# First batch of an attention-then-phase-MLP kernel loaded with two tokens per partition and put in token order by selection products; the channel weight's cast moved to another engine

**Chip, cores, metric.** One core of one Trainium2 chip. The metric is the device time of one execution in microseconds (us), the median of several; lower is better. The span of a profile (first to last instruction) is about 1.8 us shorter than the time of the same run. A second state, slower by some per cent at a lower clock, turns up in some executions of any kernel. e5 to e8 ran on chip 8, the other experiments on chip 14, each beside runs of the kernel before on its own chip. In the traces PE is TensorE, DVE VectorE, ACT ScalarE, POOL GpSimd and SP SyncE, which issues the transfers (DMA); PSUM is the memory into which PE's products go (tiles named ..._ps), and evacuation is the copy out of it.

## The reference, cut to what matters

Four batches of 768 tokens, eight heads of 64. A retention layer (a running state per head that decays by gamma and takes up k v at each token) gives x; x goes through a phase MLP whose token mixing needs all 768 tokens of a batch.

```python
for t in range(S):                       # retention
    state = gamma * state + k[t] (outer) v[t]
    y[t] = scale * q[t] @ state
x = y, heads side by side                # (4, 768, 512)
theta = x @ w_theta
zr, zi = x * cos(theta), x * sin(theta)
u = x + w_tok_r @ zr + w_tok_i @ zi      # over the tokens of one batch
out = u + relu(u @ w_ch)
```

## The kernel before: the parts that matter

A token tile is 128 tokens; there are 24, six to a batch. "Prologue" is batch 0 (tiles 0 to 5), after which a loop of slots takes a tile a slot and, beside it, the token mixing of output tiles.

```python
def load_chunk(n):                       # one tile: 64 floats = 256 bytes a row
    for name, src in (("kf", k), ("qf", q), ("vf", v)):
        t = io.tile([P, H, D], FT, name=name, bufs=9)
        nc.sync.dma_start(out=t, in_=src[b, :, c*P:(c+1)*P, :].rearrange("h s d -> s h d"))
...
def att_prep(n):                         # GpSimd: to bf16, with decay factors
    nc.gpsimd.tensor_copy(kb, kf); nc.gpsimd.tensor_mul(qb, qf, qsc); nc.gpsimd.tensor_mul(vb, vf, vsc)
def att_T(n):                            # k and q transposed, ONE VectorE copy of 128x1024
    ...
    nc.vector.tensor_copy(kqT, kq_ps)
def att_A(n):                            # k q^T of eight heads, masked, one PSUM buffer
    at_ps = psum.tile([P, 2, NP, P], FT, name="at_ps", tag="at", bufs=1)
    ...
    nc.vector.tensor_mul(at, at_ps, mask)
# att_Y: y^T and the state; att_X: x, theta, cos and sin (ScalarE); att_Z: z = x*(cos, sin) (VectorE)
...
for s_ in range(last_slot):              # the slot loop
    ...
    if s_ == 0:
        w_cast(3)
        nc.gpsimd.tensor_copy(wch, wdma["ch"])   # channel weight, 128x2048
    if s_ + 1 in n_of and n_of[s_ + 1] < N_DMA:
        att_prep(n_of[s_ + 1])           # GpSimd, behind that cast
```

## Time and profile before

| | value |
|---|---|
| time, median (3 runs) | 183.64 us (181.92 to 552.78; the last is an outlier) |
| time and span of the profiled run | 185.79 and 184.0 us |
| busy in that span: PE, VectorE, ScalarE, GpSimd | 161.1, 106.1, 72.6, 79.9 us |
| transposes of tile 6 (the prologue's last act) | 41.65 us |
| transposes of tile 8 (slot loop running free) | 54.89 us |
| from tile 6's transposes to the end | 142.35 us |

PE is busy in 88% of the span; of its 22.9 us of idle time 17.1 lie in the first 60 us and 3.9 in the last 5. Between them PE simply works, so the kernel is read by milestones: when PE starts the transposes of a given tile. Whatever delays tile 8 delays the end.

### The profile page before, as it was taken

What the parts mean: (1) busy time and instruction counts of PE and PEld (TensorE: products, weight loads), DVE (VectorE), ACT (ScalarE), POOL (GpSimd) and SP (SyncE); (2) the same over time, 40 slices, a digit from 0 to 9 for tenths busy, and PEclk for the clock granted to TensorE, in tenths of its full rate; (3) what the DMA queues carried; (4) which work ended last, traced back from release to release, by engine and by line L of the source; (5) the groups of instructions that cost most, each with busy time, mean ns of one, the idle gap of its engine ahead of it and who ended that gap; (6) DMA issues with size and microseconds to landing.
All of it is one profiled execution on the core that took longest, in us unless ns stands there. A gap on an engine that the chain in (4) does not pass through costs nothing.

```text
span 184.0 us, 3550 instructions
## 1 busy us (share of the span) xinstructions
PE 161.1 (88%) x1392; PEld 91.6 (50%) x1392; DVE 106.1 (58%) x146; ACT 72.6 (39%) x136; POOL 79.9 (43%) x105
## 2 busy tenths in 40 slices
PE   0567997795499989799999999999999999999991
PEld 0244655452265656555655565555545544444560
DVE  1264684736155877868976686756556634534442
ACT  4052754640044645554734544265354342200010
POOL 4648767691977669655859455231000000000000
PEclk9999999999579999999999999999999999999998
DMA  6999999998999989999999999954483333334343
GB/s 133 222 316 218 227 254 279 284 286 242 229 279 218 288 177 222 257 277 231 242 210 254 260 224 188 203 143 114 110 108 100 101 85 77 107 118 114 111 122 116
DMA packets 95265, 35.63 MB, mean 194 GB/s; under 512 B 89488, under 2 KB 89744, under 8 KB 95248
## 3 DMA queue, kind: packets, MB, share of 16 engines
q1 hardware_dynamic: 95104, 35.27, 85.4%
q8 instruction: 11, 0.18, 0.5%
q10 hardware_dynamic: 144, 0.13, 0.2%
q14 instruction: 6, 0.05, 0.1%
HBM read 25.69 MB, written 6.29 MB: 174 GB/s over the span
## 4 chain that ended last, share of the span: by engine, by line
PE 63%; SPq 15%; DMA 9%; DVE 5%; POOL 3%; ACT 1%; issue 1%; DVEq 0%; POOLq 0%
PE y_ps L282 29%; SPq L80 12%; PE o_ps L310 10%; PE th_ps L253 8%; DMA w<-in_moe_w_ch_dram 5%; DMA wtok<-in_moe_w_tok_r_dram 3%; PE at_ps L185 3%; PE yT_ps L214 3%; PE kq_ps L165 3%; SPq L94 2%; PE st_ps L222 2%; DVE at L189 2%; PE x_ps L250 2%; PE yT_ps L203 2%; DMA uT<-u 2%; DVE z L264 1%
## 5 line engine op out<-in xcount | busy, mean ns | idle before, releaser
L282 PE MATMUL y_ps<-z,wtr 128*128 128x512 bf16 x138 | 53.1, 385 | 1.5 <-DVE z L264 1.0
L282 PE MATMUL y_ps<-z,wti 128*128 128x512 bf16 x138 | 53.1, 385 | 0.0
L189 DVE TENSOR_TENSOR at<-at_ps,mask 128x1024 bf16<-128x1024 f32 x24 | 29.3, 1220 | 9.4 <-PE at_ps L185 9.4
L258 ACT ACTIVATE cs<-th_ps,halfpi 128x512 bf16<-128x512 f32 x24 | 16.5, 687 | 38.5 <-PE th_ps L253 38.5
L264 DVE TENSOR_TENSOR z<-cs,x_sb 128x1024 bf16<-128x1024 bf16 x24 | 20.8, 865 | 15.1 <-ACT cs L259 15.0
L154 POOL TENSOR_TENSOR kqb<-qf,qsc 128x512 bf16<-128x512 f32 x24 | 25.2, 1052 | 8.9 <-DMA qf<-in_q_dram 8.7
L156 POOL TENSOR_TENSOR vb<-vf,vsc 128x512 bf16<-128x512 f32 x24 | 25.4, 1060 | 7.5 <-PE yT_ps L214 3.3
L253 PE MATMUL th_ps<-wth,xT 128*128 128x512 bf16 x96 | 25.5, 389 | 1.9 <-DVE wth L393 1.9
L168 DVE COPY kqT<-kq_ps 128x1024 bf16<-128x1024 bf16 x19 | 13.1, 689 | 21.0 <-PE kq_ps L165 21.0
L153 POOL CAST kqb<-kf 128x512 bf16<-128x512 f32 x24 | 16.4, 684 | 18.8 <-DMA kf<-in_k_dram 8.1
L165 PE MATMUL kq_ps<-ident,kqb 128*128 128x128 bf16 x152 | 13.9, 238 | 11.7 <-POOL kqb L153 8.8
L287 DVE TENSOR_TENSOR u<-y_ps,x_sb 128x512 bf16<-128x512 f32 x23 | 15.8, 689 | 13.7 <-PE y_ps L282 13.7
L310 PE MATMUL o_ps<-wch,uT 128*128 128x512 bf16 x92 | 23.5, 380 | 0.1
L231 ACT CAST xT<-yT_ps 128x512 bf16<-128x512 f32 x24 | 14.0, 585 | 24.1 <-PE yT_ps L214 24.0
L313 DVE SCALAR_TENSOR_TENSOR ot<-o_ps,u 128x512 f32<-128x512 f32 x23 | 15.8, 690 | 10.2 <-PE o_ps L310 10.1
L282 PEld LDWEIGHTS <-wti 128*128 128x128 bf16 x138 | 13.6, 99 | 15.5 <-issue 2.6
L282 PEld LDWEIGHTS <-wtr 128*128 128x128 bf16 x138 | 13.6, 99 | 14.1 <-DVE wtr L334 0.7
L165 PEld LDWEIGHTS <-kqb 128*128 128x128 bf16 x152 | 11.0, 106 | 16.8 <-POOL kqb L153 9.2
L259 ACT ACTIVATE cs<-th_ps,zerob 128x512 bf16<-128x512 f32 x24 | 16.3, 680 | 0.0
L236 ACT CAST stbd<-st_ps 64x256 bf16<-64x256 f32 x40 | 14.7, 366 | 0.5
L295 ACT COPY uT<-u_ps 128x512 bf16<-128x512 bf16 x12 | 7.0, 585 | 18.5 <-PE u_ps L293 18.5
L310 PEld LDWEIGHTS <-uT 128*128 128x128 bf16 x92 | 8.7, 98 | 9.8 <-DMA uT<-u 0.3
(51 smaller groups left out, 149.0 us busy)
## 6 DMA issues: line engine op xcount, KB each, us to landing
kf<-in_k_dram SPq DMA_DIRECT2D x24, 256.0 KB, 4.8
qf<-in_q_dram SPq DMA_DIRECT2D x24, 256.0 KB, 5.1
vf<-in_v_dram SPq DMA_DIRECT2D x24, 256.0 KB, 5.3
out_dram<-ot SPq DMA_DIRECT2D x23, 256.0 KB, 2.2
wtok<-in_moe_w_tok_r_dram SPq DMA_DIRECT2D x6, 384.0 KB, 5.3
wtok<-in_moe_w_tok_i_dram SPq DMA_DIRECT2D x6, 384.0 KB, 5.1
w<-in_moe_w_theta_dram SPq DMA_DIRECT2D x1, 1024.0 KB, 6.7
w<-in_moe_w_ch_dram SPq DMA_DIRECT2D x1, 1024.0 KB, 8.5
```

The source lines that it names most:

```text
L80: nc.sync.dma_start(out=t, in_=src[b, :, c * P:(c + 1) * P, :].rearrange("h s d -> s h d"))
L153: nc.gpsimd.tensor_copy(kb.rearrange(r3, h=H), raw[n, "kf"])
L154: nc.gpsimd.tensor_mul(qb.rearrange(r3, h=H), raw[n, "qf"], _bcast_last(qsc[:, c], D))
L156: nc.gpsimd.tensor_mul(vb.rearrange(r3, h=H), raw[n, "vf"], _bcast_last(vsc[:, c], D))
L165: nc.tensor.transpose(kq_ps[:, i * NP + j, :], src[:, j * P:(j + 1) * P], ident)
L189: nc.vector.tensor_mul(at.rearrange("p a j t -> p (a j) t"), at_ps.rearrange("p a j t -> p (a j) t"), _bcast_mid(mask, H))
L253: nc.tensor.matmul(th_ps, s["xT"][:, j, :], wth[:, j, :], start=(j == 0), stop=(j == NP - 1))
L258: nc.scalar.activation(cs[:, 0, :], th_ps, AF.Sin, bias=halfpi, scale=1.0)
L259: nc.scalar.activation(cs[:, 1, :], th_ps, AF.Sin, bias=zerob, scale=1.0)
L264: nc.vector.tensor_mul(zs[b][:, c], st[n]["cs"], _bcast_mid(xs[b][:, c, :], 2))
L282: nc.tensor.matmul(y_ps, wT[r][:, s0, t0 * P:(t0 + 1) * P], zs[b][:, s0, r, :], start=(s0 == 0 and r == 0), stop=(s0 == nT - 1 and r == 1))
L310: nc.tensor.matmul(o_ps, mo[m]["uT"][:, j, :], wch[:, j, :], start=(j == 0), stop=(j == nD - 1))
```

## The change

The intent: rows of 512 bytes should cost the DMA engines less per byte than rows of 256. So k, q and v of batch 0 are loaded two tiles at a time, with tokens 2p and 2p+1 of 256 in partition p. For k and v the token order is restored by products with a 0/1 selection matrix (sel) into PSUM, for the transposed k and q by a copy that interleaves the even and odd tokens. v goes on ScalarE's queue. The prologue is reordered for pairs, and the cast of the channel weight goes from GpSimd in slot 0 to ScalarE in slot 2. To make room the single-tile load buffers go from 9 to 7 for each tensor and the buffers of the two 1 MB weights from 2 to 1. The diff is cut and shortened.

```diff
+    def load_pair(g, names, eng):
+                t = io.tile([P, H, 2 * D], FT, name="pair", bufs=5)
+                eng.dma_start(out=t, in_=src[0, :, 2*g*P:2*(g+1)*P, :].rearrange(
+                    "h (p two) d -> p h (two d)", two=2))
-    for what in ("c0 c1 th c2 c3 c4 w0 c5 w1 w2 c6 w3 ch c7 c8 ...
+    load_pair(0, "v", nc.scalar)
+    loads("p0 th p1 w0 p2 w1 w2 c6 w3 c7 ch c8 ...")
...
+    def pair_T(g, name):                 # for k, then for q
+        ps = psum.tile([P, NP, 2, P], BF, name="kq_ps", tag="tr", bufs=2)
+        ... transposes ...
+        nc.vector.tensor_copy(t.rearrange("d j (p two) -> d j p two", two=2),
+                              ps.rearrange("d j two p -> d j p two"))
+    def pair_rows(g, name):              # for k, then for v
+        ps = psum.tile([P, 2, dm], FT, name="r_ps", tag="at", bufs=1)
+        ... four products: sel[rows, two] with the landed rows into ps[:, a] ...
+        for a in range(2):
+            if name == "v" and a == 0: nc.vector.tensor_copy(t, ps[:, a, :])
+            else:                      nc.scalar.copy(t, ps[:, a, :])
...
+    def pair_in(g):
+        pair_prep(g, "k"); pair_T(g, "k"); pair_rows(g, "k")
+        pair_prep(g, "q"); pair_T(g, "q")
+        if g > 0: att_Z(2 * g - 1)
+        att_A(2 * g)
+        pair_prep(g, "v"); pair_rows(g, "v")
+        att_A(2 * g + 1)
+    pair_in(0); att_YS(0); ... load_pair(1, "v", nc.scalar); att_X(0); att_YS(1) ...
-            nc.gpsimd.tensor_copy(wch, wdma["ch"])          # slot 0
+        if s_ == 2: wch_cast(0, nD)                         # four ScalarE copies
-    ... O_at = ... {2: 0, 3: 1}
+    ... O_at = ... {3: 0, 4: 1}                             # o of the first two output tiles a slot later
```

More of the change, by code (lines that the diff above doesn't have):

```diff
@@ L78, in load_chunk @@
         for name, src in (("kf", k), ("qf", q), ("vf", v)):
-            t = io.tile([P, H, D], FT, name=name, bufs=9)
+            t = io.tile([P, H, D], FT, name=name, bufs=7)
             nc.sync.dma_start(
@@ L82, in load_chunk @@
             raw[n, name] = t
+    def load_pair(g, names, eng):
+        for name, src in (("k", k), ("q", q), ("v", v)):
+            if name in names:
+                t = io.tile([P, H, 2 * D], FT, name="pair", bufs=5)
+                eng.dma_start(out=t, in_=src[0, :, 2 * g * P:2 * (g + 1) * P, :].rearrange(
+                    "h (p two) d -> p h (two d)", two=2))
+                raw[g, name] = t
     wdma = {}
     def load_w512(name, src):
-        t = io.tile([P, nD, dm], FT, name="w512", bufs=2)
+        t = io.tile([P, nD, dm], FT, name="w512", bufs=1)
         nc.sync.dma_start(out=t, in_=src.rearrange("(a p) e -> p a e", p=P))
@@ L95, in load_wtok, with loads @@
         wdma[r, t0] = t
-    for what in ("c0 c1 th c2 c3 c4 w0 c5 w1 w2 c6 w3 ch c7 c8 w4 c9 c10 w5 c11 "
-                 "c12").split():
-        if what == "th":
-            load_w512("th", moe_w_theta)
-        elif what == "ch":
-            load_w512("ch", moe_w_ch)
-        elif what[0] == "c":
-            load_chunk(int(what[1:]))
-        else:
-            for r in range(2):
-                load_wtok(r, int(what[1:]))
+    def loads(order):
+        for what in order.split():
+            if what == "th":
+                load_w512("th", moe_w_theta)
+            elif what == "ch":
+                load_w512("ch", moe_w_ch)
+            elif what[0] == "w":
+                for r in range(2):
+                    load_wtok(r, int(what[1:]))
+            elif what[0] == "p":
+                load_pair(int(what[1:]), "kq", nc.sync)
+            else:
+                load_chunk(int(what[1:]))
+    load_pair(0, "v", nc.scalar)
+    loads("p0 th p1 w0 p2 w1 w2 c6 w3 c7 ch c8 w4 c9 c10 w5 c11 c12")
     posn = const.tile([P, nT], FT)
@@ L127 @@
     nc.scalar.activation(qsc, arg, AF.Exp, bias=lscale, scale=1.0)
+    posp = const.tile([P, nT], FT)
+    nc.gpsimd.iota(posp, pattern=[[2 * P, nT // 2], [1, 2]], base=1,
+                   channel_multiplier=2, allow_small_or_imprecise_dtypes=True)
+    argp = const.tile([P, nT, H], FT)
+    nc.vector.tensor_mul(argp, _bcast_last(posp, H), _bcast_mid(lg, nT))
+    vscp = const.tile([P, nT, H], FT)
+    nc.scalar.activation(vscp, argp, AF.Exp, bias=zerob, scale=-1.0)
+    qscp = const.tile([P, nT, H], FT)
+    nc.scalar.activation(qscp, argp, AF.Exp, bias=lscale, scale=1.0)
     ident = const.tile([P, P], BF)
@@ L133 @@
                             base=0, pattern=[[1, P]], channel_multiplier=-1)
+    sel = const.tile([P, 2, P], BF)
+    nc.gpsimd.memset(sel, 1.0)
+    for a in range(2):
+        half = sel[a * P // 2:(a + 1) * P // 2]
+        nc.gpsimd.affine_select(out=half, in_=half, compare_op=ALU.is_equal, fill=0.0,
+                                base=0, pattern=[[1, 2], [-1, P]], channel_multiplier=2)
     stbd = []
@@ L151, in att_prep @@
         kb, qb = kqb[:, 0, :], kqb[:, 1, :]
-        vb = work.tile([P, dm], BF, name="vb", bufs=5)
+        vb = work.tile([P, dm], BF, name="vb", bufs=8)
         nc.gpsimd.tensor_copy(kb.rearrange(r3, h=H), raw[n, "kf"])
@@ L168, in att_T @@
         nc.vector.tensor_copy(kqT, kq_ps)
-        s["kqT"] = kqT
+        s["kT"], s["qT"] = kqT[:, 0:NP, :], kqT[:, NP:2 * NP, :]
     def att_T_dma(n):
@@ L175, in att_T_dma, with pair_prep @@
             out=kqT, in_=s["kqb"].rearrange("p a d -> p (a d)"))
-        s["kqT"] = kqT
+        s["kT"], s["qT"] = kqT[:, 0:NP, :], kqT[:, NP:2 * NP, :]
+    def pair_prep(g, name):
+        t = work.tile([P, 2, dm], BF, name="kqb", bufs=5)
+        src = raw[g, name].rearrange("p h (two d) -> p two h d", two=2)
+        dst = t.rearrange("p two (h d) -> p two h d", h=H)
+        if name == "k":
+            nc.gpsimd.tensor_copy(dst, src)
+        else:
+            for two in range(2):
+                sc = (qscp if name == "q" else vscp)[:, 2 * g + two]
+                nc.gpsimd.tensor_mul(dst[:, two], src[:, two], _bcast_last(sc, D))
+        st[g, name] = t
+    def pair_T(g, name):
+        ps = psum.tile([P, NP, 2, P], BF, name="kq_ps", tag="tr", bufs=2)
+        for two in range(2):
+            for j in range(NP):
+                nc.tensor.transpose(ps[:, j, two, :],
+                                    st[g, name][:, two, j * P:(j + 1) * P], ident)
+        t = work.tile([P, NP, 2 * P], BF, name="kqT", bufs=4)
+        nc.vector.tensor_copy(t.rearrange("d j (p two) -> d j p two", two=2),
+                              ps.rearrange("d j two p -> d j p two"))
+        for a in range(2):
+            s = st.setdefault(2 * g + a, {})
+            s[name + "T"] = t[:, :, a * P:(a + 1) * P]
+    def pair_rows(g, name):
+        ps = psum.tile([P, 2, dm], FT, name="r_ps", tag="at", bufs=1)
+        for two in range(2):
+            for a in range(2):
+                rows = slice(a * P // 2, (a + 1) * P // 2)
+                nc.tensor.matmul(ps[:, a, :], sel[rows, two, :], st[g, name][rows, two, :],
+                                 start=(two == 0), stop=(two == 1),
+                                 skip_group_check=True)
+        for a in range(2):
+            t = work.tile([P, dm], BF, name="vb", bufs=8)
+            if name == "v" and a == 0:
+                nc.vector.tensor_copy(t, ps[:, a, :])
+            else:
+                nc.scalar.copy(t, ps[:, a, :])
+            st.setdefault(2 * g + a, {})[name + "b"] = t
     def att_A(n):
         s = st[n]
-        kqT = s["kqT"]
         at_ps = psum.tile([P, 2, NP, P], FT, name="at_ps", tag="at", bufs=1)
@@ L184, in att_A @@
                 rows = slice(par * D, (par + 1) * D)
-                nc.tensor.matmul(at_ps[:, par, j, :], kqT[rows, j, :],
-                                 kqT[rows, NP + j, :], start=(j == 0),
+                nc.tensor.matmul(at_ps[:, par, j, :], s["kT"][rows, j, :],
+                                 s["qT"][rows, j, :], start=(j == 0),
                                  stop=(j == NP - 1), skip_group_check=True)
@@ L203, in att_Yinter @@
                 nc.tensor.matmul(s["yT_ps"][:, j, :], stbd[c % 2][:, j, :],
-                                 s["kqT"][:, NP + j, :], start=(j == 0), stop=False,
+                                 s["qT"][:, j, :], start=(j == 0), stop=False,
                                  skip_group_check=True)
@@ L314, in moe_O, with wch_cast @@
         nc.sync.dma_start(out=out[b, t0 * P:(t0 + 1) * P, :], in_=ot)
+    def wch_cast(lo, hi):
+        for a in range(lo, hi):
+            nc.scalar.copy(wch[:, a, :], wdma["ch"][:, a, :])
     wrow = {}
@@ L382, in moe_last, with att_YS @@
                 out=out[b, t0 * P:(t0 + 1) * P, e * hw:(e + 1) * hw], in_=ot)
-    att_prep(0)
-    for n in range(nT):
-        att_T(n)
-        if n > 0:
-            att_Yinter(n - 1)
-            att_Y(n - 1)
-        att_A(n)
-        if n == 1:
-            nc.vector.tensor_copy(wth, wdma["th"])
-        if n > 0:
-            att_X(n - 1)
-        if n > 1:
-            att_Z(n - 2)
-        if n == nT - 2:
-            w_cast(0)
-        if n + 1 < nT:
-            att_prep(n + 1)
-        if n == nT - 2:
-            w_tok(0)
-            moe_M(0, 0, nT - 3)
-        if n == nT - 1:
-            moe_M(0, nT - 3, nT - 2)
+    def pair_in(g):
+        pair_prep(g, "k")
+        pair_T(g, "k")
+        pair_rows(g, "k")
+        pair_prep(g, "q")
+        pair_T(g, "q")
+        if g > 0:
+            att_Z(2 * g - 1)
+        att_A(2 * g)
+        pair_prep(g, "v")
+        pair_rows(g, "v")
+        att_A(2 * g + 1)
+    def att_YS(n):
+        att_Yinter(n)
+        att_Y(n)
+    pair_in(0)
+    att_YS(0)
+    nc.vector.tensor_copy(wth, wdma["th"])
+    load_pair(1, "v", nc.scalar)
+    att_X(0)
+    att_YS(1)
+    att_Z(0)
+    att_X(1)
+    pair_in(1)
+    w_cast(0)
+    att_YS(2)
+    load_pair(2, "v", nc.scalar)
+    w_tok(0)
+    att_X(2)
+    att_YS(3)
+    moe_M(0, 0, 2)
+    att_Z(2)
+    att_X(3)
+    pair_in(2)
+    moe_M(0, 2, 4)
     w_cast(1)
-    att_Yinter(nT - 1)
-    att_Y(nT - 1)
-    att_Z(nT - 2)
+    att_YS(4)
     w_tok(1)
+    att_X(4)
+    att_YS(5)
+    w_cast(2)
+    moe_M(1, 0, 4)
+    att_prep(nT)
+    att_Z(4)
+    att_X(5)
     moe_M(0, nT - 2, nT - 1)
-    att_X(nT - 1)
-    w_cast(2)
-    att_prep(nT)
-    moe_M(1, 0, nT - 1)
+    moe_M(1, nT - 2, nT - 1)
+    att_T(nT)
     att_Z(nT - 1)
@@ L420 @@
     moe_M(1, nT - 1, nT)
-    att_T(nT)
     n_of = {i: nT + i for i in range(NCH - nT)}
-    halves, U_at, O_at = {}, {1: 0, 2: 1}, {2: 0, 3: 1}
+    halves, U_at, O_at = {}, {1: 0, 2: 1}, {3: 0, 4: 1}
     for m in range(2, nT):
@@ L476 @@
                 att_X_dma(n_of[s_ - 1])
+        if s_ == 2:
+            wch_cast(0, nD)
         if len(hs) > 1:
```

## The prediction

> **What bounds the kernel now.** I read the busy slices of the page first, then the chain of what ended last, then the windows, then the timeline of the first 62 us. The page:
>
> ```profile
> PE   0567997795499989799999999999999999999991
> PEclk9999999999579999999999999999999999999998
> DMA  6999999998999989999999999954483333334343
> ```
>
> Each digit is a slice of 4.6 us. From slice 14 on (about 60 us) TensorE (PE) is full to the end; before that it has holes, and the DMA engines are full. So there are two stages: a start in which data arrive, and a long stage that TensorE bounds. The windows give them in numbers (length, then busy time of PE, PEld, DVE, ACT, POOL, then granted clock, DMA share, GB/s):
>
> ```profile
> 40.00:45.00 5.00, 3.95 (x40) 2.26 (x37) 3.74 (x6) 0.80 (x1) 1.74 (x2) 1.00 0.95 273
> 45.00:50.00 5.00, 1.65 (x10) 1.05 (x11) 0.60 (x2) 0.00 (x0) 4.55 (x5) 0.65 0.90 202
> 50.00:55.00 5.00, 4.67 (x45) 2.75 (x43) 2.69 (x4) 1.93 (x5) 3.68 (x5) 0.67 1.07 281
> ...
> 100.00:110.00 10.00, 10.00 (x103) 5.97 (x102) 7.22 (x11) 4.91 (x9) 5.66 (x7) 1.00 1.13 244
> ```
>
> From 45 to 50 us PE works 1.65 of 5 us and then runs at a reduced clock. The chain says why:
>
> ```profile
> 35.92 0.97 SPq L94
> 36.94 8.46 DMA w<-in_moe_w_ch_dram
> 45.45 1.89 POOL wch L457
> 47.35 0.56 POOL kqb L153
> 47.90 1.01 POOL kqb L154
> ```
>
> The channel weight lands at 45.4, GpSimd casts it for 1.89 us, and only then, in its order, prepares k and q of token tile 7, for which PE waits 4.01 us (43.95 to 47.96). What the reader should take from it: anything that moves the point at which the slot loop runs free (tile 8's transposes, 54.89 us) moves the end by as much, because PE has only about 2 us of idle time after it, until the last transfer at 175. So the sum has to be made at 54.89 us.
>
> Earlier, the first batch is paced by arrivals. The GB/s of 25 us in slices of 0.625:
>
> ```profile
> GB/s 0 0 0 121 260 277 244 222 225 220 217 219 211 224 247 338 383 396 355 285 249 223 217 218 218 218 218 218 217 217 220 217 217 218 241 230 270 388 417 283
> ```
>
> The flats of 217 are q, k and v in 256-byte rows; the rise to 338 to 396 is the 2 KB rows of the theta weight, 388 to 417 the 3 KB rows of the token weights. One tile then takes about 3.3 us, as the theta products of tiles 1, 2 and 3 show:
>
> ```profile
> 19.62 1.03 PE L253 MATMUL th_ps<-wth,xT 128*128 128x512 bf16 x4
> ...
> 22.98 1.03 PE L253 MATMUL th_ps<-wth,xT 128*128 128x512 bf16 x4
> ...
> 26.23 1.03 PE L253 MATMUL th_ps<-wth,xT 128*128 128x512 bf16 x4
> ```
>
> 3 x 256 KB at 217 GB/s is 3.6 us: arrival, not work, is the pace. Before: X(5), the last theta product of the batch, begins at 37.09, the loop (slot 0) at 42.16.
>
> **What the Trainium skill says.** "DMA: Bandwidth & Descriptors", section Specifications, gives 512 B or more as the transfer for line rate. The trace shows only the trend: 217 GB/s over 16 engines is 18.9 ns for a 256-byte packet; 370 for 2 KB rows is 88.6 ns; a line through both gives 28.9 ns for 512 B, so 284 GB/s, an estimate, not the full 380. The same page, "Issuing engines are not separate DMA queues", says that another issuing queue saves only issue time; so putting v on ScalarE's queue adds no bandwidth, and in program order it can even issue late. No run shows this yet. "TensorE: Matmul & The Clock Gate", "What's actually happening": about 3.4 us of idling halves the clock and as much work restores it. The trace agrees: after the idle 4.01 us the products at 50 us are 0.43 us apart, against 0.215 later, and the early ones were also 0.43 apart until 19 us. "VectorE: DVE Perf Modes", Mode 2x_1P: two 16-bit elements per cycle need step 1. The trace agrees in so far as 1024 bf16 elements from PSUM take 0.689 us below and 1024 f32 ones 1.220.
>
> ```profile
> L189 DVE TENSOR_TENSOR at<-at_ps,mask 128x1024 bf16<-128x1024 f32 x24 | 29.3, 1220 | 9.4 <-PE at_ps L185 9.4
> L154 POOL TENSOR_TENSOR kqb<-qf,qsc 128x512 bf16<-128x512 f32 x24 | 25.2, 1052 | 8.9 <-DMA qf<-in_q_dram 8.7
> L168 DVE COPY kqT<-kq_ps 128x1024 bf16<-128x1024 bf16 x19 | 13.1, 689 | 21.0 <-PE kq_ps L165 21.0
> L287 DVE TENSOR_TENSOR u<-y_ps,x_sb 128x512 bf16<-128x512 f32 x23 | 15.8, 689 | 13.7 <-PE y_ps L282 13.7
> L231 ACT CAST xT<-yT_ps 128x512 bf16<-128x512 f32 x24 | 14.0, 585 | 24.1 <-PE yT_ps L214 24.0
> ```
>
> **The change part by part.**
>
> *Gain 1, rows.* Six tiles are 4.7 MB: 21.7 us at 217, 16.6 us at 284. 5.1 us of DMA time saved, if the DMA stays the pace.
>
> *Gain 2, the weight's cast.* It moves to ScalarE in slot 2, so GpSimd is not held. Worth at most the 4.01 us wait, 0.4 us for q, and the slow clock: slot 1 took 6.93 us (47.96 to 54.89); its products at full clock (transposes 0.45, six products 1.29, uT 0.22, at 0.33, yT and st 0.67, weight transposes 0.67) are 3.65. So 3.3 us besides the wait.
>
> *Cost, the chain within a pair.* k rows, A of the even tile, v rows and A of the odd tile all use one PSUM buffer, so each waits for the evacuation of the one before. Per pair: k rows 0.6 (four 512-column products, two row halves at once), two ScalarE copies 2 x 0.585 = 1.2, A 0.4, mask 1.22, v rows 0.55, copy 0.69, A 0.4, mask 1.22: 6.3 us, with little other PE work placed in between. The old way had 2 x (0.4 + 1.22) = 3.2. The two transposed copies now read PSUM with a stride of 128, so I take 1.2 rather than 0.69 each.
>
> *Pass through the first pair.* First bytes at 2.15 as before. v0 shares the engines, so 512 KB of k lands near 6.3 (before: 256 KB at 4.1), q near 8.8. GpSimd k 1.15 to 7.5; q 2 x 1.05 to 10.9; v to 13.0. Transposes of q done 11.6, copy 12.8, A 13.5, mask 14.7, v rows 15.7, copy 16.4, A 17.0, mask 18.3; yT and st 18.0, ScalarE xT and state to 18.9; theta cast on VectorE to 19.6; theta product at half clock to 21.5; tile 1's Y, then ScalarE cos, sin, xT to 23.4; X(1) ends near 25 (before 20.7).
>
> *Pair 1.* v1 is issued by ScalarE only after tile 0's state, at 19, and lands near 23.5, GpSimd ready 25.6, in time. Copies of kT and qT to 28, A 28.5, mask 30.1, v rows and copy 31.4, A 31.9; Y(2), weight transposes, X(2), Y(3), four products, X(3) about 5.7: 37.6 (before 27.3).
>
> *Pair 2.* Same 7 us chain to 44.5, then products 0.9, Y(4) 0.8, weight transposes 0.8, X(4) 1.1, Y(5) 0.6, eight products 1.7, X(5) 1.1: 51.3. Then products, transposes of tile 6 and of w2: slot 0 at 54.5 against 42.16. Slot 0 needs 1.6, slot 1 3.65: tile 8 at 59.8 against 54.89, 4.9 us later.
>
> So gain 1 is hidden: the SyncE queue even runs dry, because w2 waits for the casts of w0, which GpSimd does behind v1 (about 26 us), and w3 for those of w1, behind v2 (about 40 us). From there 17 tiles of 3.6 us plus weights are still under PE's pace. After slot 2 PE's work is the same; some of the old 2 us of idling may go, I count 0.5. Sum: 183.64 + 4.9 - 0.5 = 188.0 us.
>
> **The rivals.** (a) Arrival was the whole bound and the pairs' chain is short: copies at 0.69, k at 5.5, q at 7.8. Running the same pass, X(1) ends at 23.2, X(3) at 35.1, slot 0 at 51.1 and tile 8 at 56.4: still +1.5, so 185. For it: the flats of 217. Against: the single PSUM buffer. For a real gain (179), the passes would have to be 4 us too long besides. (b) The clock: between the pairs PE is busy under a third of some 5 us, so it may fall to half speed in each; 2 to 3 us more, 191. For it: what happened at 46 us. Against: only 1.6 us idle at a stretch. (c) The late w3, tile 7 and channel weight turn into a new DMA wait in slots 1 to 5: each tile is 3.6 us and slots are 5 to 6, but tile 9 and w4 come only just in time; plus 1 to 3 us, 191.
>
> **Range and chances.** Centre 188.0. Rival (a) is the low side, (b) and (c) the high side: 184.5 to 193. Slower than 187.3 is 2%: 0.57. Within: 0.33. Faster than 180.0 asks that the serial chain be wrong by 8 us in all: 0.10.
>
> **What would show it.** Right: tile 8's transposes near 60 us; PE idle in three blocks between 10 and 45 us, put down to VectorE's copies and mask; kT copies near 1.2 us; GB/s near 284 in the first 20 us, then gaps near 24 and 37 us; no wait on the channel weight. Wrong: tile 8 before 55, GB/s above 330 on the pair loads, copies at 0.69, or X(1) ending before 21.

## The result, and the profile after

The changed kernel takes 202.14 us (201.28 to 202.28, 4 runs), the kernel before 184.09 (all but the outlier between 181.92 and 184.54, 4 runs). The ratio is 1.101, 95% interval 1.091 to 1.112: slower by 10%. (Ratios here are the mean time of one kernel's fast runs over that of the other's of the same rounds, so not quite the ratio of the medians.) The direction was predicted, the size was not: 202.1 lies well above the range of 184.5 to 193.

The busy slices of the changed kernel's page, 5.0 us to a digit:

```profile
PE   0436863983987999897999999999999999999992
...
PEclk9999997596699999999999999999999999999999
DMA  5999739309999999999699856999455434324443
```

PE now fills up only at slice 14, some 65 us; the DMA row has holes at slices 6, 8 and 9, where before it was full; and the clock row, which dipped once before, dips twice (slices 7 to 8 and 10 to 11). (The row does not show the start: it reads full there, yet the theta products of tiles 0 and 1 took 1.86 and 1.91 us, at half the later pace, until 26 us; in the kernel before, until 19. At the start, go by the length of the products.) The transposes of tiles 6 and 8 on PE's timeline (start, length), in the kernel before and then in the changed one:

```profile
41.65 0.61 PE L165 MATMUL kq_ps<-ident,kqb 128*128 128x128 bf16 x8
...
54.89 0.61 PE L165 MATMUL kq_ps<-ident,kqb 128*128 128x128 bf16 x8 [0.33 <-DVE wtr L334]
```

```profile
60.99 0.61 PE L197 MATMUL kq_ps<-ident,kqb 128*128 128x128 bf16 x8
...
70.86 0.61 PE L197 MATMUL kq_ps<-ident,kqb 128*128 128x128 bf16 x8 [0.48 <-DVE wtr L413]
```

X(n) is the theta product of tile n, A(n) its k q^T; the times are from the timelines, the predicted ones from the prediction's pass.

| milestone, us | before | predicted | after |
|---|---|---|---|
| X(1) ends (first pair through) | 20.65 | 25 | 26.3 |
| X(3) ends | 27.3 | 37.6 | 42.7 |
| X(5) ends | 38.1 | 51.3 | 60.3 |
| tile 6's transposes | 41.65 | | 60.99 |
| slot 0 begins | 42.16 | 54.5 | 64.85 |
| tile 8's transposes | 54.89 | 59.8 | 70.86 |
| end of span | 184.0 | | 200.4 |

Tile 8 is 16.0 us later and the end 16.4: the rule held, and the loss is made in the prologue. (The median times differ by 18.05, since the profiled run of the kernel before, at 185.79, was itself 1.70 us over the median of 184.09.) The windows of the prologue (length, busy time of PE, PEld, DVE, ACT, POOL, granted clock, DMA share, GB/s):

```profile
30.00:35.00 5.00, 1.89 (x20) 1.10 (x22) 2.98 (x4) 0.58 (x1) 1.41 (x1) 0.80 0.93 223
35.00:40.00 5.00, 4.99 (x40) 3.36 (x38) 1.56 (x3) 2.46 (x5) 0.00 (x0) 0.52 0.37 105
40.00:45.00 5.00, 4.24 (x44) 2.31 (x43) 3.14 (x4) 4.21 (x9) 4.73 (x5) 1.00 0.08 20
45.00:50.00 5.00, 1.66 (x18) 0.73 (x20) 2.97 (x4) 0.61 (x2) 0.06 (x1) 0.66 0.97 258
```

First PE stands (1.89 of 5 us busy), then it is busy without a hole (4.99 of 5) at half clock, while DMA idles. The chain of what ended last in pair 1 (start, length, what), from the end of X(1):

```profile
26.78 1.13 DVE kqT L231
...
27.93 1.22 DVE kqT L231
29.14 1.37 DVE z L339
30.51 1.15 DVE at L264
...
31.70 0.62 PE r_ps L243 x4
...
32.35 0.70 DVE vb L249
...
33.08 0.59 ACT vb L251
...
33.71 0.61 PE at_ps L260 x8
...
35.97 1.28 PE w_ps L407 x12
...
37.85 1.71 PE th_ps L328 x4
```

Not one DMA stands in it: what was an arrival-paced prologue is now a relay between VectorE, PE and ScalarE. And at its end, twelve 128-column transposes take 1.28 us and a theta product 1.71; at full clock the same theta products took 0.86 in this kernel's chain, at 41.84 us.

DMA did what was hoped. The GB/s of the first 25 us in slices of 0.625:

```profile
GB/s 0 0 0 96 122 320 348 322 292 291 292 289 315 367 377 396 368 333 295 290 289 290 337 359 398 367 336 295 289 291 289 327 369 398 376 329 292 161 0 0
```

The flats of 217 have become flats of 289 to 292, and then the queue runs dry.

### The profile page after: what moved, and what is told of

It is laid out like the page before. It is cut to its first block, busy times and chain, and to the rows that moved or that the text cites. A ratio compares the mean times of both kernels' runs of the same rounds, so it can differ in the third digit from the quotient of the medians.

```text
span 200.4 us, 3618 instructions
## 1 busy us (share of the span) xinstructions
PE 168.6 (84%) x1416; PEld 94.3 (47%) x1416; DVE 110.9 (55%) x150; ACT 79.6 (40%) x151; POOL 77.5 (39%) x105
## 4 chain that ended last, share of the span: by engine, by line
PE 73%; DVE 14%; ACT 5%; DMA 4%; issue 1%; POOL 1%; DVEq 0%; SPq 0%; ACTq 0%; POOLq 0%
PE y_ps L357 29%; PE th_ps L328 11%; PE o_ps L385 10%; DVE at L264 5%; PE at_ps L260 4%; DMA pair<-in_q_dram 4%; PE yT_ps L289 3%; DVE kqT L231 3%; PE x_ps L325 3%; PE st_ps L297 2%; PE kq_ps L197 2%; DVE z L339 2%; PE yT_ps L278 2%; ACT cs L333 1%; PE r_ps L243 1%; PE y_ps L427 1%
## 5 line engine op out<-in xcount | busy, mean ns | idle before, releaser
L339 DVE TENSOR_TENSOR z<-cs,x_sb 128x1024 bf16<-128x1024 bf16 x24 | 19.8, 827 | 22.4 <-ACT cs L334 22.4
L328 PE MATMUL th_ps<-wth,xT 128*128 128x512 bf16 x96 | 27.2, 410 | 0.6 <-DVE wth L483 0.6
L185 POOL CAST kqb<-kf 128x512 bf16<-128x512 f32 x18 | 11.4, 635 | 23.6 <-PE st_ps L297 13.2
L188 POOL TENSOR_TENSOR vb<-vf,vsc 128x512 bf16<-128x512 f32 x18 | 20.1, 1115 | 0.0
L186 POOL TENSOR_TENSOR kqb<-qf,qsc 128x512 bf16<-128x512 f32 x18 | 19.2, 1065 | 0.5 <-DMA qf<-in_q_dram 0.5
L260 PE MATMUL at_ps<-kqT 64*128 64x128 bf16 x192 | 10.4, 232 | 8.3 <-ACT vb L251 4.2
L400 POOL CAST wrow<-wtok 128x768 bf16<-128x768 f32 x12 | 10.2, 862 | 17.6 <-issue 16.7
L311 ACT CAST stbd<-st_ps 64x256 bf16<-64x256 f32 x40 | 14.7, 367 | 0.5
L200 DVE COPY kqT<-kq_ps 128x1024 bf16<-128x1024 bf16 x13 | 9.0, 691 | 8.1 <-PE kq_ps L197 8.1
L328 PEld LDWEIGHTS <-xT 128*128 128x128 bf16 x96 | 9.2, 104 | 8.6 <-issue 2.4
```

What stands on the lines that cost most here:

```text
L186: nc.gpsimd.tensor_mul(qb.rearrange(r3, h=H), raw[n, "qf"], _bcast_last(qsc[:, c], D))
L188: nc.gpsimd.tensor_mul(vb.rearrange(r3, h=H), raw[n, "vf"], _bcast_last(vsc[:, c], D))
L260: nc.tensor.matmul(at_ps[:, par, j, :], s["kT"][rows, j, :], s["qT"][rows, j, :], start=(j == 0), stop=(j == NP - 1), skip_group_check=True)
L328: nc.tensor.matmul(th_ps, s["xT"][:, j, :], wth[:, j, :], start=(j == 0), stop=(j == NP - 1))
L339: nc.vector.tensor_mul(zs[b][:, c], st[n]["cs"], _bcast_mid(xs[b][:, c, :], 2))
```

## The experiments

"T6" is the start of tile 6's transposes: 60.99 us in the changed kernel, 41.65 before. From T6 to the end the versions of the changed kernel hardly differ (138.2 to 139.9 us in the traces of fast runs; 142.35 in the kernel before), so T6 says what the prologue costs. The same prologue, traced four times (the changed kernel, e12, e13, e14), had T6 between 59.57 and 61.16: a difference under 1.6 us between two traces says nothing.

**e2: rows in PSUM tiles of their own.** Each row half gets a one-bank tile of another pool instead of sharing the single two-bank buffer with A.

```diff
-        ps = psum.tile([P, 2, dm], FT, name="r_ps", tag="at", bufs=1)
+        ps = [psum.tile([P, dm], FT, name="r_ps", tag="acc", bufs=2) for _ in range(2)]
 ... ps[:, a, :] becomes ps[a] in the products and copies ...
```

> The changed kernel with the selection products in two one-bank tiles of the accumulator buffers instead of the two-bank buffer of A. Theory of the serial chain: the odd tile's A no longer waits for the mask, the v rows and the two copies one after another, about 2.0 us less per pair (33.71 to 31.7 us in pair 1), so 6 us less in all, 195 to 197 us, more if the clock recovers too. Theory of late data (v issued late on ScalarE's queue, SyncE's queue stalled): v lands as late as before, so within 1 us of 202.

Measured 195.26 us (ratio 1.058), T6 54.57: 6.4 us off the prologue from moving one buffer. In the changed kernel ScalarE's copy of the odd tile's v stood behind VectorE's copy of the even tile's, because both halves were one tile to the program:

```profile
16.60 0.58 ACT L251 CAST vb<-r_ps 128x512 bf16<-128x512 f32 x1 [6.23 <-DVE vb L249]
```

In e2 these two copies start at 14.50 and 14.87 us, side by side. So the serial use of one PSUM buffer is a real cause (how much of the 6.4 us is the waits and how much the clock, which still fell in e2 but for less long, this run does not part).

**e3: a plain copy of the transposed pair** (wrong: the tokens stay out of order).

```diff
-        nc.vector.tensor_copy(t.rearrange("d j (p two) -> d j p two", two=2),
-                              ps.rearrange("d j two p -> d j p two"))
+        nc.vector.tensor_copy(t, ps.rearrange("d j two p -> d j (two p)"))
```

> The changed kernel with the copy of the transposed k and q left in the order in which they stand in PSUM, wrong on purpose (tokens stay in the wrong order). Theory of the serial chain: the copy falls from 1.22 to 0.69 us, two of them per pair stand in the chain, 6 x 0.53 = 3.2 us less: 198 to 199.5 us. Theory of late data: within 1 us of 202.

Measured 198.32 us (1.078), T6 56.76: 4.2 us less. The two interleaving copies per pair do cost, 1.22 us each against 0.69 for the plain ones.

**e4: dummy products that keep PE busy** (18 products of 512 columns in each pair, into a buffer nobody reads).

```diff
+            nc.tensor.matmul(w_ps, ident, sel_w, start=True, stop=True, ...)   # warm(5), warm(8), warm(5)
```

> The changed kernel with 18 idle products of 512 columns per pair put where TensorE waits in the pair (5 before the even A, 8 after it, 5 after the v rows). If the halved clock is a large part of the loss: the clock stays at 1.00 from about 25 us on, and two stretches of some 6 us at half speed and part of the start go, 5 to 7 us less: 195 to 197 us. If the clock is only a sign of the waiting: 201 to 205 us, as the added products come on top.

Measured 197.43 us (1.072), T6 56.29: 4.7 us less although PE does more. The windows of e4, the same columns:

```profile
30.00:35.00 5.00, 4.65 (x49) 2.46 (x48) 2.93 (x4) 1.60 (x4) 1.40 (x2) 1.00 0.98 219
45.00:50.00 5.00, 4.47 (x50) 2.59 (x47) 2.47 (x3) 1.85 (x5) 0.57 (x1) 1.00 1.09 248
```

The clock is 1.00 where it was 0.80 and 0.66. So the halved clock alone was worth at least 4.7 us, more than the 2 to 3 us of rival (b).

**e5: v of pairs 1 and 2 issued early**, by SyncE right behind k and q.

```diff
-    loads("p0 th p1 w0 p2 w1 w2 ...")
+    loads("p0 th p1 v1 w0 p2 v2 w1 w2 ...")
...
-    load_pair(1, "v", nc.scalar)     # and the same for pair 2
```

> The changed kernel with all v pairs issued by SyncE right after their k and q, instead of by ScalarE after the first tile of the pair before. Theory of late data: GpSimd's waits of 7.3 and 8.9 us for v go, the gaps in the DMA at 25 to 30 and 38 to 47 us close, and 6 us or more go: 196 or less. Theory of the serial chain: the gaps close as well, but the v rows are held by the mask and not by v, so 200.5 to 203 us.

Measured 200.42 us (1.087), T6 60.29. The profile gives 0.7 us, which is within the spread of T6; the time 1.7 against the changed kernel's 202.14, but 0.7 against its second measurement below (e13, 201.15). Late v is not the cause. DMA had idled because SyncE's queue waited for buffers (22.0 us in the changed kernel for GpSimd's casts of the token weights, 14.7 in e5), and PE did not yet need what was held up. The gaps at 25 to 30 and 40 to 45 us closed (314 and 264 GB/s), but not the one at 35 to 40 (115), and a new one came at 50 to 55 (52).

**e6: e2, e3 and dummies at once** (wrong).

> The changed kernel with the three edits together that each gave something: selection products in their own banks, plain copy (wrong on purpose), and 14 idle products per pair. The single gains were 6.9, 3.8 and 4.7 us, 15.4 in sum. If they are separate causes: 187 us. As all three shorten or fill the same waits I expect part of them to be the same time: 188 to 192. If the loss had another cause: above 193.

Measured 197.7 us (1.072), T6 56.57: a miss: about as e3 or e4 alone, and worse than e2 alone. The experiment was badly made. Its chain in pair 1 says so:

```profile
27.92 0.73 PE warm_ps L484 x3
...
29.42 1.19 PE warm_ps L484 x5
```

Once the waits that hid them were gone, the dummies themselves were on the path. It says nothing on whether the causes add, so it was made again without them:

**e9: e2, e3 and e5 together, no dummies** (wrong).

> Wrong on purpose (the token order is not restored in the copies of kT and qT). The changed kernel with three things at once and no dummy products: both row halves in separate one-bank PSUM tiles, plain copies of the transposed pair instead of the strided ones, and v of pairs 1 and 2 issued by SyncE right behind k and q. Theory (the pass through a pair is one serial chain, so what each edit takes off the chain adds up: 6 us and 4 us in the profile alone, 0.7 for v): the loop's tile 6 transposes near 50.5 to 51.5 us instead of 60.99, and a time near 190 to 192. Rival (the edits shorten the same wait, or the arrival of the next data takes over, so they do not add): tile 6 no earlier than 53.5, time 195 or above.

Measured 190.18 us (1.036), T6 49.13. The single gains, 6.4, 4.2 and 0.7, would have given 49.6: within the spread of T6 they add. The windows of e9:

```profile
30.00:35.00 5.00, 4.61 (x44) 2.70 (x45) 1.75 (x4) 3.75 (x8) 1.33 (x2) 1.00 1.03 267
35.00:40.00 5.00, 2.73 (x33) 1.42 (x34) 3.56 (x5) 2.56 (x5) 0.00 (x0) 1.00 1.16 288
45.00:50.00 5.00, 4.48 (x33) 2.60 (x34) 1.47 (x3) 2.15 (x4) 1.96 (x2) 1.00 1.11 285
```

From 21 us on the clock never falls, without a single dummy: with the shorter waits it stayed up. So the 11.9 us that e9 takes off the prologue include what the halved clock cost; the clock is not a third cause beside the two waits but an amplifier of them. e9 beside e6 also shows what e6's dummies cost: up to 7.4 us at T6 (e9 has v early too, which was worth 0.7 alone).

**e7: a correct mend.** e2 and e5, with kT's copy on ScalarE and qT's on VectorE, and the next pair's transposes and rows placed among the products of the pair before.

```diff
+        (nc.scalar.copy if name == "k" else nc.vector.tensor_copy)(t..., ps...)
+    pk(0); pq(0); att_A(0); pv(0); att_A(1); pk(1); att_YS(0); ...; pq(1); ...; att_A(2); ...; pv(1); att_A(3) ...
```

> A correct mend of the changed kernel: selection products in their own banks, v issued early, the copies of kT on ScalarE, and the rows and transposes of the next pair placed among the products of this one. Theory of the serial chain: tile 8's transposes near 56 to 59 us instead of 70.9, so 185 to 190 us. Below 181 it would beat the kernel before. If the added work itself (selection products, strided copies) is the cost and not its place: 194 or more.

Measured 192.75 us (1.045), correct, T6 51.63. Half of the loss is back, but it still loses to the kernel before. Its clock falls once more, so:

**e11: e7 with 16 dummies** around the rows and A of pair 2.

> Correct. The mended kernel (e7, pipelined pairs) with 16 dummy products (6, 6 and 4) around the v rows and A of pair 2, where e7's clock fell to half from 39.8 to 46 us. Theory (what is left there is in part the halved clock): the clock at 1.0 in 40 to 50 us, tile 6 transposes 2 to 3 us earlier than e7's 51.63, time 189.5 to 191. Rival (the chain of copies and waits alone sets it, the products lie in its shadow): tile 6 within 1 us of 51.63, time within 1 us of 192.75 or above it.

Measured 193.07 us (1.051), T6 51.46: no gain. The window of e7, then that of e11, and a line of e11's chain:

```profile
40.00:45.00 5.00, 4.44 (x35) 3.27 (x35) 1.05 (x2) 1.92 (x4) 1.15 (x2) 0.50 1.15 272
```

```profile
40.00:45.00 5.00, 4.36 (x47) 2.43 (x45) 2.25 (x3) 1.06 (x3) 0.34 (x1) 1.00 1.07 251
```

```profile
39.01 1.46 PE warm_ps L485 x6
```

The clock rose from 0.50 to 1.00, but 1.46 us of dummies lay on the path. The outcome is the rival's, yet it doesn't prove the rival: gain and cost cancelled. The token-mixing products that start at 40.55 us in e7 start at 42.71 in e11, but the theta products after them end at 46.62 and 46.45.

**e10: reordering for nothing** (wrong: rows are used as they landed, no selection products, plain copies, v early; the sines' argument scaled by 0.1 to stay in range; two work buffer counts differ).

```diff
+            st.setdefault(2 * g + a, {})[name + "b"] = st[g, name][:, a, :]     # in place of products and copies
```

> Wrong on purpose (rows of a pair are used as they landed, no selection products at all; the argument of the sines is scaled by 0.1 so that it stays in range). The changed kernel with the 512-byte pair loads, the deferred channel weight cast and v early, but with the reordering for nothing. It tells what the wider rows could give at the best. Theory (the cost is the reordering, and the wider rows are worth little since X(1) needs k and q of two tiles before anything can start): tile 6 transposes near 45 to 47 us, time 184 to 188, the same as before within 2%. Rival (the wider rows are worth the 5 us of DMA time that I counted, and only the reordering hides it): tile 6 at or before 38, time at or below 179.

Fast runs 187.27 to 187.45 us; ratio 1.019, interval 1.014 to 1.025. Two of five runs, the profiled one among them, took 192.2 and 193.1 and count as slow, so only the fast times are used. Measured by 2% the verdict is "unclear", but the interval lies above 1: in this schedule the wide rows do not pay even with the token order for nothing, and the rival, that they are worth 5 us once the reordering is free, falls for it. e10 is e9 without the selection products and their copies: 187.45 against 190.18 us, so these cost 2.7 us. The run keeps the changed kernel's order by pairs, its fewer load buffers and the moved cast, so a pipelined schedule (as in e7) with free reordering, or the old buffers, stays untested.

**e1: the kernel before, with only the channel weight's cast moved** to ScalarE in slot 2.

```diff
-            nc.gpsimd.tensor_copy(wch, wdma["ch"])
+        if s_ == 2:
+            wch_cast(0, nD)
-    halves, U_at, O_at = {}, {1: 0, 2: 1}, {2: 0, 3: 1}
+    halves, U_at, O_at = {}, {1: 0, 2: 1}, {3: 0, 4: 1}
```

> The kernel before with one part of the change alone: the channel weight cast by ScalarE in slot 2 instead of GpSimd in slot 0, and the first two output products one slot later. If that part is a gain hidden under a loss elsewhere: TensorE's 4.0 us wait at 44 us and most of the slow clock after it go, so 177 to 180 us and a granted clock of 1.00 from 45 to 55 us. If this part is what made the changed kernel slow: above 186 us.

Measured 184.1 us against 184.21 (ratio 0.997, interval 0.988 to 1.005): not resolved. Its profile has tile 8 at 50.92, 4.0 us earlier than before's, and a span of 180.9; but the runs of the kernel before beside it had spans of 180.9 to 183.6 themselves, without a trace to say why. What the times leave of the 4 us stays open.

**e8: e1 with tile 7 loaded ahead of the channel weight**, five rounds.

> The kernel before with the channel weight cast by ScalarE in slot 2 and loaded after tile 7 instead of before it. If tile 7's arrival was the rest of the wait at 44 us: TensorE has no wait over 1 us there and the time is 1 to 3 us under the kernel before, 180.5 to 183 us. If the DMA engines, full until 118 us, take the gain back later: within 1 us of it, as with the cast alone (ratio 0.997).

Measured 185.2 us (1.004, interval 0.998 to 1.010): the same. Tile 8 came at 50.06, but PE then waited 1.52 and 1.02 us for its k and q, which GpSimd could prepare only when DMA had brought them: a wait on the DMA queue in place of another.

**e12: the changed kernel with the cast back** on GpSimd in slot 0: the reverse of e1's diff, applied to the changed kernel.

> Correct. The changed kernel with one part undone: the channel weight is cast by GpSimd in slot 0 again, before it prepares token tile 7, and o of the first two output tiles comes one slot earlier again. Theory (the deferred cast, my gain 2, is worth in the changed kernel what its trace shows: 139.4 us from tile 6's transposes to the end against 142.35 before): tile 6 unchanged near 61, from there to the end 142 to 145, time 204.5 to 208. Rival (in the changed kernel the loop starts so late that the channel weight would have landed in time anyway, so that the cast costs only its own 1.9 us on an idle GpSimd): from tile 6 to the end within 1 us of 139.4, time 201.3 to 203.2.

Measured 199.66 us (1.086): faster than the changed kernel, against both theories. The cast on GpSimd as the trace lists it (line, duration min/median/max, first and last start), with no idle time before it:

```profile
L553 POOL CAST wch<-w x1: 2349/2349/2349, 61.4 to 61.4; 128x2048 bf16<-128x2048 f32 x1
```

With a prologue 18 us longer than in the kernel before, the weight is there when GpSimd wants it, so there is no wait to remove. And the chain of the changed kernel shows what ScalarE's casts cost:

```profile
75.22 2.18 ACT wch L393 x4
...
77.41 0.69 ACT cs L333
78.09 0.59 ACT cs L334
...
78.72 1.98 PE o_ps L385 x8
```

They hold up cos and sin of a tile, whose PSUM buffer PE then waits for: 0.20 us before these o products, a wait that e12 doesn't have. At PE's next two waits it stands 0.89 and 1.31 us against 0.58 and 0.93 in e12. Together that is 0.9 us; the rest of the 1.2 us below is not placed. Since 1.4 us of the difference lay before T6, where the two programs are the same, both were run again side by side:

**e13: the changed kernel again; e14: e12 again.** Five rounds, one chip.

> The changed kernel as it is, again, on the chip of the next three runs, for comparison with them. Theory (the deferred cast costs only what lies after tile 6's transposes, 1.2 us, and the rest of e12's gain is the difference between two chips or two profiles): 200.3 to 201.2, tile 6 near 60. Rival (the recorded 202.1 holds on this chip too, so the cast costs 2.5 us, part of it before the loop): 201.6 to 202.6, tile 6 near 61.

> The same kernel as e12 (channel weight cast by GpSimd in slot 0 again), beside e13. Theory: 199.0 to 200.0 as in e12, 1.2 us under e13 give or take 0.5. Rival: 2.0 to 3.0 under e13. A third outcome, the same as e13 within 0.5, would mean that e12's gain was the chip alone.

e13: 201.15 us (1.094), T6 61.16; e14: 200.42 (1.090), T6 60.05. The median times are 0.7 us apart, with intervals that overlap. From T6 to the end it is 139.4 us in the changed kernel and in e13, 138.2 in e12 and e14.

**e15: e10 with the cast back; e16: e7 with the cast back.**

> Wrong on purpose, as e10 (no reordering, sines of a tenth of the argument), with the channel weight cast by GpSimd in slot 0 again. Theory (the deferred cast helps only when the loop starts before the channel weight is there; here the loop starts at 46 in a fast run, a little after it did before, so the weight is late again and the cast waits): within 1 us of e10's fast 187.4 or slower. Rival (the cast on ScalarE is a cost here too): 184.9 to 186.3, one to two and a half under e10, so the same as the kernel before within 1 per cent.

> Correct. The mended kernel e7 with the channel weight cast by GpSimd in slot 0 again. Theory (the two causes are separate; the loop starts at 51.6, the weight lands at about that time): 191 to 193, at most 1.2 us under e7's 192.75. Rival (the weight is late for this earlier loop, and the wait for it is back): 193.5 to 196.

e15: fast runs 188.35 to 188.5 us (1.025), no better than e10; its profile is slow. e16: 190.63 us (1.037), a little under the 191 to 193 expected; correct, and the best correct version of the change. (Of the 2.1 us under e7, 1.2 lie before T6, where the two programs are the same.) From T6 to the end: 138.6 in e16 against 139.8 in e7. So in three like-for-like comparisons of traces the deferred cast costs 1.2 us from T6 to the end; in the times that is resolved only in part, since the length of the prologue varies from run to run by as much. No version beats the kernel before.

## Why the prediction was right or wrong

**Right: the mechanism.** The end follows tile 8, and the prologue's pass through the pairs sets it: +16.0 and +16.4 us. After the first pair arrivals ceased to matter, as the sum said (gain 1 hidden, the queue dry): no DMA stands in pair 1's chain, and v early (e5) gives nothing that is resolved. The rate (289 to 292 GB/s against 284 predicted), the interleaving copy (1.22 us against 1.2) and the issue of v of pair 1 at 19 us were right:

```profile
19.08 0.38 ACTq L89 DMA_DIRECT2D pair<-in_v_dram  x1
```

**Wrong: the size, in the steps "Pair 1" and "Pair 2".** The error at tile 8 is 70.86 − 59.8 = 11.1 us. By the milestones: first pair +1.3, pair 1 +3.8 (16.4 against 12.6), pair 2 +3.9 (17.6 against 13.7), from X(5) to slot 0 +1.4 (4.6 against 3.2), slots 0 and 1 +0.7. The terms of pair 1, from its chain:

| term | predicted | measured |
|---|---|---|
| copies of kT and qT, with their transposes | 3.0 | 2.8 (26.30 to 29.14) |
| A, z and mask | 2.1 | 2.5 (to 31.66) |
| v rows, copies, A | 1.8 | 2.7 (to 34.32) |
| the rest to the end of X(3) | 5.7 | 8.4 (to 42.70) |

The largest miss is the last row: of the 8.4 us, the 5.2 from 34.32 to 39.55 are PE work without a hole at half clock, about 2.6 at full clock by that ratio. The prediction had this as rival (b), with 2 to 3 us for all, and kept it out of the centre on the argument that PE was "only 1.6 us idle at a stretch". The trace has idle stretches of 1.36, 2.11 and 1.41 us with bursts of 0.4 to 0.6 us between, and the clock fell all the same. e4 puts it at 4.7 us or more. The next miss, the third row, is the serial evacuation: I counted 0.69 us for both v copies as if they ran side by side, while the program orders them (0.70 + 0.59). e2 shows that the single buffer as a whole was worth 6.4 us with the clock that follows from it. Pair 2 repeats both: the work from 50.38 to 53.67 us ran at half clock, and v's copies again took 0.70 + 0.59 in turn. The smaller rest is waits I left out, such as cos and sin ahead of the products of pair 2 (1.3 us at 56.0).

**Right number, wrong reason: gain 2.** Slots 0 and 1 up to tile 8 did shrink, from 12.7 us to 6.0 (predicted 5.3). I put this down to the moved cast. e12 has the cast back and the same 6.0: in the changed kernel the late loop alone removes the wait, and the move costs 1.2 us later. I had taken a gain worked out for the old schedule into the new one without asking whether the wait would still be there.

**The last 2.1 us, and two slips.** I added my difference to the median of 183.64 but took it from a profiled run of 185.79. Together: 4.4 predicted, 16.4 measured in the profiles, 18.5 over that median. The terms of pair 2 as listed give 51.5, not 51.3, and those of slot 1 give 3.63, not 3.65; neither matters.

What stays open: why even the kernel with free reordering (e10) loses 1.9%, since its only profile is of a slow run. It is not a fall of the clock like that in pair 1: the three fast runs had a mean granted clock of 0.997 or 0.998 over the whole span, no lower than the kernel before (0.979 to 0.995 in its fast runs beside the experiments). Pairs need two tiles' k and q before anything starts, and the work is bunched, but this is argued, not shown. And how short an idle stretch has to be for the clock to hold: 2.73 us busy of 5 kept it in e9 (35 to 40), and 2.79 of 5 in the same stretch of e7 was followed by half clock; a longest idle stretch of 1.50 us kept it in e9's pair 1, and one of 1.45 us did not in e2's.

## What to carry to other kernels

When a change makes the transfers cheaper by adding work between engines, lay the new chain out engine by engine, with each shared buffer as a wait, before counting the bytes saved. A relay of short waits can cost twice, once as idle time and again because PE's clock falls, as here, where the next 5.2 us of work ran at half speed; take that into the centre of an estimate, not into a rival. And ask of each gain whether the wait that it removes still exists once the rest of the change has moved the schedule.

## What the Trainium skill lacked or had wrong

- "TensorE: Matmul & The Clock Gate", section "What's actually happening", which I used, ties the half clock to an idle window of about 3.4 us. Read as one unbroken stretch, that is not enough: here no idle stretch of pair 1 was longer than 2.11 us and the clock fell to 0.52 in the window that followed. The same page's section "A second HAM failure mode: psum-queue depth-cycling" does tell of short idles between groups of products that make the clock oscillate; the runs agree with that one. It gives no measure of how much idling is enough; here neither the busy share of 5 us (2.73 and 2.79) nor the longest idle stretch (1.50 and 1.45 us) told which kernel would keep its clock.
- "DMA: Bandwidth & Descriptors", section Specifications, gives 512 B as the least transfer for line rate. Rows of 512 bytes ran at 289 to 292 GB/s, between the 217 of 256-byte rows and the 338 to 396 of 2 KB rows: better, not yet the full rate; that row alone promises too much.
